# One kernel's hand-written order of steps replaced from end to end: softmax attention with a highway layer, eight batches on one core

## The chip, the cores and the metric

The kernel runs on one NeuronCore of a Trainium2 chip. The metric is the device time of one execution in microseconds; before the change its median is 117.8 us over 3 runs (117.66 to 118.46). A profile is taken of one further execution, and all instruction times below come from it. The engines are named as in the profile: PE (TensorE's matmuls), PEld (its weight loads), DVE (VectorE), ACT (ScalarE), POOL (GpSimd) and SP (the engine that issues most DMAs).

## The reference

```python
q, k, v: (8, 8, 576, 64) float32          # batch, heads, positions, head size
q_s = softmax(q, over the head size)
k_s = softmax(k, over the positions)
kv  = einsum('bhsd,bhse->bhde', k_s, v)   # 64x64 for each head
a   = einsum('bhsd,bhde->bhse', q_s, kv)
x   = a.transpose(0, 2, 1, 3).reshape(4608, 512)
H   = relu(x @ w_h)
T   = sigmoid(x @ w_t + b_t)
out = T * H + (1 - T) * x                 # (4608, 512) float32
```

## The kernel before

The 4608 rows are cut into 36 tiles of 128 rows. A pair of batches makes nine tiles: four of the first batch, four of the second, and one that holds the last 64 rows of both (tile numbers 8, 17, 26 and 35). Each batch has a preparation, and each tile a chain of steps. The program is a flat list of such steps, the string ORDER (line 16 on), written out by hand; the loop at line 502 runs through it and calls one small function for each entry. An entry `mt_17_0` is step mt for tile (or batch) 17, part 0; a letter behind a colon says which engine does it (A is ScalarE, D VectorE, P GpSimd; F joins two halves in one instruction). Nothing else orders the work: each engine executes its own instructions strictly in the order in which the list names them, waits where an operand or a buffer is not ready, and everything behind a waiting instruction on that engine waits too.

Preparation of batch b. `q`, `k`, `v` are loads issued by SP (lines 184, 200, 204, 208); each tensor has three landing buffers, so a load waits until batch b-3 has been consumed. `ek` (line 255) is exp of k, `eq` (300, 304, 309) exp of q, both on ScalarE. `vc` (261) casts v to float16 on GpSimd, ScalarE or VectorE. `kv` (271) accumulates the 64x64 products and the column sums in PSUM, `kr` (283) takes the reciprocals and `kn` (289) writes the normalized block to SBUF, both on VectorE. `qt` (321, 326) transposes exp(q) on TensorE, `qc` (335) copies the result to SBUF. For batch 7 alone, `qd` (342) does this with two DMA transposes.

Chain of tile i. `xu` (363) multiplies the transposed exp(q) with kv. `rs` and `x` (372, 378, VectorE) divide by the row sums. `xt` (386) transposes x on TensorE, `xe` (393) copies it to SBUF on VectorE or ScalarE. `bw` (401 on ScalarE, 403 on TensorE) puts the bias into a PSUM bank, `mt` (413) adds x @ w_t to it, `mh` (421) forms x @ (w_h/2 - I/2) in another bank (the identity is taken from w_h by `whd`, line 228, and the halving is in the cast `whc`, line 234; `wtc`, line 224, casts w_t). `th` (435, 437) is tanh on ScalarE, `dd` (441) is max(gps, -x/2) on VectorE. `uu` forms (tanh+1)*d either in one VectorE instruction (455) or, for tiles marked P, in two GpSimd instructions (452, 453); in the first case the PSUM bank is free only after uu, in the second already after th. `oo` (473, GpSimd) adds x. `st` (481, 489, 493) stores; for most tiles one store takes the halves of two neighbouring tiles. Tiles 0, 4, 5, 6 and 7 do xu to xe and the matmuls in two halves. `fill` (168) are matmuls on zeros that are executed while the first loads are under way.

PSUM's eight banks: two for bw/mt, two for mh (and for the xu of halved tiles), one pair for xu and kv, one for qt, one for the transposes. In SBUF, x has six buffers, d, u, th and the transposed x three each, a pair of output tiles seven, a single output tile three. In the built program each DMA of SP also waits until the eighth DMA before it has landed.

Of the kernel before, what the change touches and what calls it, by code (L numbers as in the profile page):

```python
# [31 lines left out]
uu_6_0:P oo_8_0 oo_6_0 xe_9_0:D mh_7_0 dd_7 bw_7:A mt_7_1 mt_7_0 xu_10_0 xt_12_0 mh_9_0 xe_12_0:D rs_10_0 q_3_0 x_10_0
eq_3_0 eq_3_1 qt_3_2 qc_3_2 dd_9 mh_12_0 xt_10_0 xe_10_0:D qt_3_1 qc_3_1 k_3_0 th_7_0 bw_10:A v_3_0 vc_3_0 xu_11_0
rs_11_0 bw_9:A mt_9_0 ek_3_0 ek_3_2 dd_12 vc_3_2:A x_11_0 qt_3_0 th_9_0 qc_3_0 uu_7_0:P oo_7_0 uu_9_0 mt_10_0 th_10_0
bw_12:A kv_3_0 qt_2_2 q_4_0 qc_2_2:A mh_10_0 eq_4_0:F kr_3_0 kn_3_0 xt_11_0 xe_11_0:D mt_12_0 dd_10 uu_10_0:P oo_9_0
oo_10_0 xu_14_0 rs_14_0 x_14_0 th_12_0 uu_12_0 oo_12_0 mh_11_0 qt_4_0 bw_11:A xu_13_0 rs_13_0 x_13_0 v_4_0 vc_4_0
# [10 lines left out]
dd_21 xt_22_0 xe_22_0 xu_24_0 mt_21_0 mh_22_0 xt_23_0 rs_24_0 qc_6_0 x_24_0 vc_6_0:A kv_6_0 qt_6_1 th_19_0 uu_19_0:P
oo_20_0 q_6_9 dd_22 xe_23_0:D mh_23_0 kr_6_0 th_21_0 uu_21_0 oo_19_0 kn_6_0 bw_22:A mt_22_0 qc_6_1:A dd_23 xu_25_0
rs_25_0 x_25_0 eq_5_2 xt_24_0 qt_5_2 bw_23:A mt_23_0 th_22_0 oo_21_0 uu_22_0:P oo_22_0 qc_5_2:A xu_26_0 xe_24_0
rs_26_0 x_26_0 bw_24:A th_23_0 uu_23_0 xt_25_0 mh_24_0 dd_24 st_10_1 q_7_0 oo_23_0 v_7_0 st_10_0 vc_7_0 vc_7_2 k_7_0  # L50
# [485 lines left out]
```

## Time and profile before

| | before |
|---|---|
| median of 3 runs | 117.8 us (117.66 to 118.46) |
| profiled execution | 117.78 us |
| its span | 116.0 us |
| TensorE's granted clock | 0.99 of full speed |
| data moved | 40.58 MB, 350 GB/s on average |
| DMA issues of loads of 1152 KB | 11.3 (v) and 11.8 us (k) from issue to landing |
| chain that ended last, by engine | PE 54%, POOL 26%, DVE 6%, issue 6% |

The page gives busy time for each engine, the span in 40 equal slices (2.9 us each) with the busy share in tenths, and the DMA queue's share. A matmul's row in the profile lasts longer (379 ns for 512 columns) than the distance to the next one, because matmuls overlap; so TensorE's load is read from the starts. The same holds in a smaller measure for the other engines: a row of 0.68 us on VectorE is followed by the next after 0.60. The timelines give start, duration and, in brackets, the idle time before an instruction and what ended it.

### The profile page before, as it was taken

How to read it: one execution, taken by the hardware profiler on the slowest of the kernel's cores; microseconds unless marked ns; L12 is line 12 of the kernel's file. 1: busy time of each engine (PE TensorE's matmuls, PEld its weight loads, DVE VectorE, ACT ScalarE, POOL GpSimd, SP SyncE). 2: the span in 40 equal slices, each digit the busy share in tenths (PEclk: the TensorE clock that was granted, in tenths of full speed). 3: DMA queues.
4: the chain of work that ended last, by engine and by line, in shares of the span. 5: the costliest groups of instructions: out<-in, count | busy, mean ns of one | idle time of the engine just before them, and what ended most of it. 6: DMA issues, size and time to landing. Idle time of an engine off the chain costs nothing.

```text
span 116.0 us, 3454 instructions
## 1 busy us (share of the span) xinstructions
PE 109.2 (94%) x1355; PEld 62.8 (54%) x1355; DVE 93.7 (81%) x231; ACT 91.2 (79%) x139; POOL 90.9 (78%) x103
## 2 busy tenths in 40 slices
PE   5999999999999999999999999999999999999930
...
DVE  5544678588999999998999899989789869789770
ACT  4354473997999999999999999997999796585620
POOL 5024247089998999999999999986999979999960
...
DMA  2999999999999999999999999999999999894965
GB/s 49 375 397 379 407 391 378 390 377 367 384 384 379 390 393 366 367 393 355 349 386 388 363 401 406 391 384 332 370 398 376 148 276 394 343 364 166 401 257 181
DMA packets 24755, 40.58 MB, mean 350 GB/s; under 512 B 5410, under 2 KB 12834, under 8 KB 24740
## 3 DMA queue, kind: packets, MB, share of 16 engines
...
## 4 chain that ended last, share of the span: by engine, by line
PE 54%; POOL 26%; DVE 6%; issue 6%; DMA 2%; ACT 1%; POOLq 1%; ACTq 0%
POOL o L473 14%; PE gps L421 14%; PE tps L413 13%; PE turned L168 10%; POOL u L453 6%; PE kv L271 4%; PE xu L363 4%; PE turned L386 4%; PE qps L326 3%; POOL g L452 3%; DMA out_dram<-o 2%; POOL v L261 2%; DVE x L378 2%; DVE d L441 2%; DVE xT L393 1%
## 5 line engine op out<-in xcount | busy, mean ns | idle before, releaser
L473 POOL TENSOR_TENSOR o<-u,x 128x512 f32<-128x512 f16 (+1 forms) x36 | 40.5, 1142 | 2.1 <-DVE u L455 1.2
L413 PE MATMUL tps<-w16t,xT 128*128 128x512 f16 (+1 forms) x148 | 37.2, 373 | 0.0
L421 PE MATMUL gps<-w16h,xT 128*128 128x512 f16 x144 | 36.9, 379 | 0.0
L378 DVE TENSOR_TENSOR x<-xu,rs 128x512 f16<-128x512 f32 (+1 forms) x41 | 25.5, 624 | 2.5 <-POOL g L452 0.5
L441 DVE SCALAR_TENSOR_TENSOR d<-x,gps 128x512 f16<-128x512 f16 x36 | 24.1, 677 | 0.5 <-PE gps L421 0.4
L453 POOL TENSOR_TENSOR u<-g,d 128x512 f16<-128x512 f16 x19 | 21.9, 1155 | 1.6
L261 POOL CAST v<-v 128x576 f16<-128x576 f32 (+1 forms) x14 | 12.6, 906 | 11.4 <-DMA v<-in_v_dram 11.3
L255 ACT ACTIVATE ek<-k 128x576 f16<-128x576 f32 (+2 forms) x21 | 18.8, 930 | 2.6 <-DMA k<-in_k_dram 2.5
L413 PEld LDWEIGHTS <-xT 128*128 128x128 f16 x148 | 13.4, 98 | 10.7 <-ACT xT L393 0.2
L421 PEld LDWEIGHTS <-xT 128*128 128x128 f16 x144 | 12.9, 98 | 10.9 <-DVE xT L393 0.8
L401 ACT COPY tps<-ball 128x512 f32<-128x512 f32 x29 | 16.8, 590 | 2.4 <-DVE u L455 2.1
L363 PE MATMUL xu<-kvb,eq 128*128 128x130 f16 (+1 forms) x160 | 15.4, 225 | 0.3 <-DVE x L378 0.2
L363 PEld LDWEIGHTS <-eq 128*128 128x128 f16 (+1 forms) x160 | 10.4, 100 | 8.4 <-DVE x L378 3.6
L386 PE MATMUL turned<-idh,x 128*128 128x128 f16 x144 | 14.5, 220 | 0.1
L309 ACT ACTIVATE qe<-q 128x1024 f16<-128x1024 f32 (+2 forms) x11 | 9.5, 896 | 5.3 <-DMA q<-in_q_dram 5.3
L386 PEld LDWEIGHTS <-x 128*128 128x128 f16 x144 | 10.2, 98 | 6.1 <-DVE x L378 1.6
L455 DVE SCALAR_TENSOR_TENSOR u<-tps,d 128x512 f16<-128x512 f32 (+1 forms) x17 | 11.4, 668 | 2.5 <-ACT tps L437 1.9
L168 PE MATMUL turned<-blank 128*128 128x512 f16 x45 | 12.1, 420 | 1.3 <-POOL blank L150 1.3
L452 POOL TENSOR_SCALAR g<-th 128x512 f16<-128x512 f16 x19 | 11.7, 618 | 1.2 <-DVE x L378 1.2
L435 ACT ACTIVATE th<-tps 128x512 f16<-128x512 f32 x19 | 11.2, 592 | 1.7 <-PE tps L413 1.6
L393 DVE COPY xT<-turned 128x512 f16<-128x512 f16 (+1 forms) x28 | 10.6, 384 | 2.3 <-PE turned L386 2.3
L437 ACT ACTIVATE tps<-tps 128x512 f32<-128x512 f32 (+1 forms) x18 | 10.0, 556 | 2.4 <-PE tps L413 2.4
...
## 6 DMA issues: line engine op xcount, KB each, us to landing
...
k<-in_k_dram SPq DMA_DIRECT2D x5, 1152.0 KB, 11.8
v<-in_v_dram SPq DMA_DIRECT2D x5, 1152.0 KB, 11.3
...
```

Source lines behind the costliest of these rows:

```text
L168: nc.tensor.matmul(spare, blank[:, 0:P], blank, start=True, stop=True, skip_group_check=True)
L255: nc.scalar.activation(t[:, :, c:c + n].rearrange("p j c d -> p c j d"), T[f"k32{b}"][:, c:c + n].rearrange("p c (j d) -> p c j d", j=NJ), ...
L363: nc.tensor.matmul(dst, turned_q(b, jp, n), kvb[b % NKV][:, hh, kk], start=True, stop=True, skip_group_check=True)
L378: nc.vector.tensor_mul(t[:, k0:k1], sums(i, k)[:, :, :, 0:64], T[f"rs{i}_{k}"][:, 0:k1 - k0].unsqueeze(3).to_broadcast([P, k1 - k0, 4, D]))
L386: nc.tensor.matmul(t[:, n], T[f"x{i}"][:, n0 + n % 2:n0 + 2 * P:2], idh, is_transpose=True, start=True, stop=True, skip_group_check=True)
L401: nc.scalar.copy(t[:, cs], ball[:, cs])
L413: nc.tensor.matmul(T[gate(i, k)][:, cs], T[f"xT{i}"][:, n], w16["t"][:, n, cs], start=False, stop=(n == parts[-1] and not first), skip_gro ...
L421: nc.tensor.matmul(t, T[f"xT{i}"][:, n], w16["h"][:, n], start=(first and n == parts[0]), stop=(n == parts[-1] and not (first and len(part ...
L441: nc.vector.scalar_tensor_tensor(t, T[f"x{i}"], -0.5, T[f"gps{i}"], op0=ALU.mult, op1=ALU.max)
L452: nc.gpsimd.tensor_scalar(g, T[f"th{i}"], 1.0, 1.0, op0=ALU.add, op1=ALU.mult)
L453: nc.gpsimd.tensor_mul(t, g, T[f"d{i}"])
L473: eng.tensor_add(t[:, cs], T[f"u{i}_{h}"][:, cs], T[f"x{i}"][:, cs])
```

## The change

Only the string ORDER differs; tiles, loads, halves, buffers and all functions stay. The whole sequence of entries is another one, and for some entries the engine is another one.

- The head: TensorE's fills, the bias product (`bp`) and the DVE set-up now come ahead of the first q; w_h's first half is the second load (it was the ninth); batch 0 begins with heads 2 and 3; k_1_2 and v_1_2 are loaded ahead of q_1_0. There are 46 fills instead of 45.
- vc: 9 on ScalarE (6 before), 11 on GpSimd (14), 2 on VectorE (2). qc: 5 on ScalarE (9), 17 on VectorE (13). xe: 12 on ScalarE (13), 29 on VectorE (28). bw: 29 on ScalarE and 8 on TensorE, as before.
- uu: 19 on GpSimd and 18 on VectorE, as before, but for other tiles (0, 1, 9, 13, 16, 23, 28 move to GpSimd; 2, 6, 10, 14, 17, 30, 33 to VectorE).
- eq_3, eq_5 and ek_3 are joined, eq_4 and ek_5 are split in two.
- SP: five stores come ahead of k_6_0 (three before), q_6_0 comes behind it; q_7_9 comes directly behind q_7_0, v_7_0 directly ahead of the DMA transposes; in the tail st_30, st_21, st_25, st_31, st_33, st_28, st_16_1, st_32, st_34, st_35 is the order.

The diff, cut to its head, some rows in the middle and its end:

```diff
--- before.py
+++ after.py
 ORDER = """
-setuppool q_0_0 v_0_0 fill_8 fill_8 b_32 b_0 eq_0_0 k_0_0 ek_0_0 qt_0_0 setupdve bsplit bp bc fill_8 ek_0_1 vc_0_0:D
-v_0_1 vc_0_1 kv_0_0 kr_0_0 k_0_2 fill_8 ek_0_3 v_0_2 v_0_3 vc_0_2 qc_0_0 kn_0_0 xu_0_0 vc_0_3 ek_0_2 kv_0_1 kr_0_1
-kn_0_1 q_0_4 fill_5 eq_0_1 eq_0_2 xu_1_0 rs_1_0 rs_0_0 x_1_0 x_0_0 fill_8 xt_1_0 xe_1_0:D qt_0_1 w_h_0 whd_1:P whd_0:P
-whc_0:A qc_0_1 xt_0_0 xu_0_1 rs_0_1 x_0_1 bw_1 xe_0_0 xu_3_0 rs_3_0 x_3_0 qt_0_2 bw_0 w_h_2 whd_2:P whd_3:P whc_2:A
-w_t_2 wtc_2:P xt_0_1 mh_0_0 xe_0_1:D xu_2_0 xt_3_0 xe_3_0 rs_2_0 w_t_0 wtc_0:P mh_1_0 q_1_0 mh_0_1 qc_0_2:A x_2_0
-xt_2_0 dd_1 dd_0 k_1_2 eq_1_0 v_1_2 mt_1_0 th_1_0 uu_1_0 vc_1_3 oo_1_0 ek_1_2 ek_1_3 xe_2_0:D mt_0_1 mt_0_0 th_0_0
...
-eq_1_1 xt_5_0 qt_1_1 rs_4_0 x_4_0 mh_5_1 q_2_0 eq_2_0 k_2_2 rs_8_0 xe_5_0:D qc_1_1:A x_8_0 ek_2_3 xt_4_0 xt_4_1
-xe_4_0:D xe_4_1:D mh_5_0 dd_5 mt_5_0 th_5_0 uu_5_0:P k_2_0 ek_2_1 bw_8:A ek_2_2 xu_6_0 rs_6_0 x_6_0 mt_4_1 xt_8_0
-xe_8_0:D xu_6_1 rs_6_1 qt_2_0 x_6_1 xu_7_0 rs_7_0 x_7_0 mt_4_0 xt_6_0 xu_7_1 rs_7_1 xt_6_1 xe_6_0:D xe_6_1:D x_7_1
...
-mt_13_0 dd_13 k_4_0 ek_4_0 ek_4_2 q_4_9 kv_4_0 kr_4_0 kn_4_0 th_14_0 uu_14_0:P bw_17:A th_13_0 uu_13_0 xt_15_0 xe_15_0
-qt_4_1 qc_4_1 mt_17_0 xu_18_0 rs_18_0 x_18_0 oo_14_0 q_5_0 eq_5_0 oo_13_0 v_5_0 vc_5_0 bw_15:A vc_5_2 mh_17_0 xt_16_0
-xe_16_0:D dd_17 eq_4_2 eq_5_1 mt_15_0 th_15_0 xu_20_0 qt_4_2 k_5_0 rs_20_0 x_20_0 mh_15_0 th_17_0 uu_17_0:P oo_17_0
...
-mt_16_0 th_16_0 bw_18:A qt_5_1 kv_5_0 eq_6_0:F dd_16 kr_5_0 kn_5_0 uu_16_0 bw_20:A xt_19_0 mh_18_0 qc_5_1:A st_1_0
...
-mt_20_0 xu_22_0 dd_18 uu_18_0 oo_18_0 st_5_0 st_7_1 q_5_9 st_5_1 xt_21_0 rs_22_0 x_22_0 th_20_0 dd_20 uu_20_0:P
...
-mt_24_0 xe_25_0 eq_6_2 xu_27_0 qt_6_2 xt_26_0 mh_25_0 rs_27_0 x_27_0 xe_26_0:D xu_29_0 rs_29_0 bw_25:A mt_25_0 st_17_0
-eq_7_0:F qd_7_0 qc_6_2:A dd_25 th_24_0 qd_7_1 x_29_0 xt_27_0 xe_27_0 uu_24_0 oo_24_0 mh_26_0 dd_26 xu_30_0 rs_30_0
-th_25_0 x_30_0 st_12_0 uu_25_0:P mh_27_0 bw_27:A mt_27_0 st_14_1 dd_27 xt_30_0 xu_28_0 rs_28_0 q_7_9 st_12_1 bw_26:A
...
-uu_29_0 qc_7_2:A oo_29_0 x_32_0 xe_33_0 mt_31_0 mh_33_0 xt_32_0 bw_33:A th_31_0 dd_31 st_8_0 st_19_0 st_26_0 xu_34_0
-xe_32_0 uu_31_0 rs_34_0 mt_33_0 x_34_0 oo_28_0 st_28_0 st_30_0 oo_31_0 st_31_0 st_25_0 mh_32_0 xu_35_0 dd_33 xt_34_0
-bw_32:A mt_32_0 th_33_0 uu_33_0:P oo_33_0 dd_32 xe_34_0:D mh_34_0 rs_35_0 x_35_0 xt_35_0 bw_34:A th_32_0 uu_32_0 dd_34
-xe_35_0 mt_34_0 th_34_0 uu_34_0 oo_32_0 st_33_0 st_32_0 oo_34_0 st_34_0 bw_35_0 mh_35_0 dd_35 mt_35_0 th_35_0 uu_35_0
-oo_35_0 bw_35_1 mt_35_1 st_35_0 th_35_1 uu_35_1 oo_35_1:D st_35_1:A
+setuppool fill_8 b_0 fill_8 b_32 setupdve bsplit bp fill_8 fill_8 q_0_0 w_h_0 v_0_2 vc_0_2:D whd_1:P eq_0_0 qt_0_0
+k_0_2 whd_0:P whc_0:A v_0_3 vc_0_3:A ek_0_3 ek_0_2 kv_0_1 kr_0_1 fill_8 v_0_1 k_0_0 ek_0_1 qc_0_0 kn_0_1 xu_0_1 rs_0_1
+x_0_1 v_0_0 vc_0_1 ek_0_0 vc_0_0:A kv_0_0 q_0_4 eq_0_2 eq_0_1 fill_6 kr_0_0 kn_0_0 xu_0_0 xt_0_1 rs_0_0 x_0_0 xu_1_0
+rs_1_0 xe_0_1 x_1_0 qt_0_1 xt_0_0 qc_0_1 bc bw_0 bw_2 xe_0_0 xt_1_0 w_h_2 whd_2:P mh_0_0 whd_3:P whc_2:A xu_2_0
+xe_1_0:D rs_2_0 x_2_0 mh_0_1 dd_0 mh_1_0 w_t_2 wtc_2:P w_t_0 wtc_0:P xt_2_0 xe_2_0 qt_0_2 xu_3_0 rs_3_0 mt_0_1 mt_0_0
+mh_2_0 k_1_2 ek_1_2 th_0_0 dd_1 x_3_0 mt_2_0 ek_1_3 v_1_2 vc_1_2:A vc_1_3:D uu_0_0:P oo_0_0 q_1_0 dd_2 xt_3_0 xe_3_0:D
...
+rs_4_0 xu_8_0 rs_8_0 x_4_0 qt_1_1 q_2_0 eq_2_0 qc_1_1:A xt_5_0 xe_5_0:D x_8_0 k_2_0 ek_2_1 ek_2_0 mh_5_1 xt_4_0 xt_4_1
+xe_4_1:D mh_5_0 xe_4_0:D dd_5 mt_5_0 th_5_0 xt_8_0 xu_6_1 rs_6_1 x_6_1 mt_4_1 xu_6_0 k_2_2 v_2_2 vc_2_2 ek_2_2 vc_2_3
+mt_4_0 th_4_0 bw_8:A rs_6_0 x_6_0 xu_7_0 ek_2_3 rs_7_0 x_7_0 xe_8_0:D qt_2_0 mh_4_1 mh_4_0 qc_2_0 xt_6_1 xt_6_0 xu_7_1
+xe_6_1:D rs_7_1 xe_6_0:D mt_8_0 xt_7_0 kv_2_1 v_2_0 vc_2_0 vc_2_1:A kv_2_0 dd_4 x_7_1 xt_7_1 uu_5_0:P kr_2_0 oo_5_0
...
+xu_17_0 rs_17_0 x_17_0 qt_4_1 v_4_0 vc_4_0 xt_13_0 xe_13_0:D mh_14_0 th_10_0 ek_4_0 uu_10_0 oo_10_0 dd_14 q_4_9 q_5_0
+k_5_0 vc_4_2 st_1_1 v_5_0 st_3_0 q_6_9 st_5_1 st_3_1 xu_15_0 rs_15_0 x_15_0 st_1_0 xt_17_0 mh_13_0 bw_13:A bw_14:A
+mt_14_0 xe_17_0 ek_4_2 th_14_0 k_6_0 q_5_9 v_6_0 st_5_0 dd_13 xu_16_0 rs_16_0 x_16_0 xt_15_0 mt_13_0 th_13_0 xe_15_0:D
+bw_17:A kv_4_0 qc_4_1 uu_11_0:P oo_11_0 eq_5_0:F uu_14_0 uu_13_0:P oo_14_0 kr_4_0 kn_4_0 oo_13_0 bw_15:A xt_16_0
+xe_16_0:D mh_17_0 dd_17 mt_17_0 xu_18_0 rs_18_0 x_18_0 th_17_0 uu_17_0 vc_5_2 oo_17_0 mh_15_0 mt_15_0 xt_18_0 xu_20_0
...
+oo_23_0 xe_26_0:D bw_25:A th_24_0 eq_7_2 mh_24_0 eq_7_0:F v_7_0 qd_7_0 qd_7_1 x_27_0 mt_25_0 dd_24 uu_24_0 oo_24_0
+vc_7_0 xu_30_0 mh_26_0 rs_30_0 x_30_0 xt_27_0 xe_27_0:D st_14_1 mh_25_0 xu_28_0 dd_26 th_25_0 rs_28_0 xt_30_0 dd_25
+uu_25_0:P oo_25_0 x_28_0 bw_27:A mt_27_0 st_19_0 st_12_0 st_12_1 st_14_0 st_8_0 st_23_0 xe_30_0:D bw_26:A mt_26_0
...
+dd_31 bw_33:A mt_31_0 th_31_0 uu_28_0:P st_30_0 oo_28_0 xu_34_0 rs_34_0 xt_32_0 xe_32_0:D x_34_0 uu_31_0 st_21_0
+oo_31_0 st_25_0 st_31_0 mh_33_0 mt_33_0 xu_35_0 dd_33 rs_35_0 th_33_0 uu_33_0 xt_34_0 xe_34_0:D bw_32:A mh_32_0
+mt_32_0 mh_34_0 oo_33_0 bw_34:A st_33_0 x_35_0 dd_32 th_32_0 uu_32_0 xt_35_0 mt_34_0 th_34_0 xe_35_0:D mh_35_0 st_28_0
+st_16_1 oo_32_0 st_32_0 bw_35_0 bw_35_1 mt_35_0 dd_34 uu_34_0 oo_34_0 st_34_0 th_35_0 mt_35_1 th_35_1 dd_35 uu_35_0
+oo_35_0 st_35_0 uu_35_1 oo_35_1:D st_35_1:A
 """
```

More of the change, by code (lines that the diff above doesn't have):

```diff
@@ L22 @@
-xt_2_0 dd_1 dd_0 k_1_2 eq_1_0 v_1_2 mt_1_0 th_1_0 uu_1_0 vc_1_3 oo_1_0 ek_1_2 ek_1_3 xe_2_0:D mt_0_1 mt_0_0 th_0_0
-qt_1_0 qc_1_0 mh_3_0 bw_2 mt_2_0 vc_1_2:A kv_1_1 uu_0_0 oo_0_0 th_2_0 bw_3 mt_3_0 k_1_0 ek_1_1 ek_1_0 dd_3 kr_1_1
-v_1_0 vc_1_0 vc_1_1:A kn_1_1 xu_5_1 th_3_0 rs_5_1 x_5_1 mh_2_0 dd_2 uu_2_0:P uu_3_0:P oo_2_0 oo_3_0 xt_5_1 xu_4_1
-kv_1_0 kr_1_0 rs_4_1 bw_5 kn_1_0 xe_5_1 mt_5_1 x_4_1 q_1_4 eq_1_2 xu_5_0 rs_5_0 qt_1_2 qc_1_2 bw_4 xu_4_0 xu_8_0 x_5_0
-eq_1_1 xt_5_0 qt_1_1 rs_4_0 x_4_0 mh_5_1 q_2_0 eq_2_0 k_2_2 rs_8_0 xe_5_0:D qc_1_1:A x_8_0 ek_2_3 xt_4_0 xt_4_1
@@ L27 @@
-xe_4_0:D xe_4_1:D mh_5_0 dd_5 mt_5_0 th_5_0 uu_5_0:P k_2_0 ek_2_1 bw_8:A ek_2_2 xu_6_0 rs_6_0 x_6_0 mt_4_1 xt_8_0
-xe_8_0:D xu_6_1 rs_6_1 qt_2_0 x_6_1 xu_7_0 rs_7_0 x_7_0 mt_4_0 xt_6_0 xu_7_1 rs_7_1 xt_6_1 xe_6_0:D xe_6_1:D x_7_1
-mt_8_0 ek_2_0 v_2_0 vc_2_0:D qc_2_0 mh_4_1 mh_4_0 xt_7_0 dd_4 xt_7_1 th_4_0 vc_2_1 kv_2_0 v_2_2 vc_2_3 vc_2_2:A kv_2_1
-kr_2_1 mh_8_0 bw_6:A mh_6_1 th_8_0 mt_6_1 kr_2_0 oo_5_0 kn_2_1 uu_4_0:P kn_2_0 xu_9_0 dd_8 q_2_4 eq_2_2 eq_2_1 xe_7_1
-uu_8_0:P oo_4_0 rs_9_0 x_9_0 mt_6_0 xe_7_0 qt_2_1 qc_2_1 th_6_0 mh_6_0 dd_6 mh_7_1 xt_9_0 xu_12_0 rs_12_0 x_12_0
@@ L32 @@
[L32 to L36, printed above, removed]
@@ L37 @@
-xt_14_0 xe_14_0:D vc_4_2:A bw_14:A mt_11_0 th_11_0 xu_17_0 rs_17_0 x_17_0 qc_4_0:A xt_13_0 mh_14_0 dd_11 uu_11_0:P
-oo_11_0 xu_15_0 rs_15_0 xe_13_0:D x_15_0 mt_14_0 dd_14 mh_13_0 xu_16_0 rs_16_0 x_16_0 bw_13:A xt_17_0 xe_17_0:D
-mt_13_0 dd_13 k_4_0 ek_4_0 ek_4_2 q_4_9 kv_4_0 kr_4_0 kn_4_0 th_14_0 uu_14_0:P bw_17:A th_13_0 uu_13_0 xt_15_0 xe_15_0
-qt_4_1 qc_4_1 mt_17_0 xu_18_0 rs_18_0 x_18_0 oo_14_0 q_5_0 eq_5_0 oo_13_0 v_5_0 vc_5_0 bw_15:A vc_5_2 mh_17_0 xt_16_0
-xe_16_0:D dd_17 eq_4_2 eq_5_1 mt_15_0 th_15_0 xu_20_0 qt_4_2 k_5_0 rs_20_0 x_20_0 mh_15_0 th_17_0 uu_17_0:P oo_17_0
@@ L42 @@
-xt_18_0 mh_16_0 xu_19_0 dd_15 qc_4_2 xe_18_0:D rs_19_0 qt_5_0 qc_5_0 bw_16:A ek_5_0:F xt_20_0 x_19_0 q_6_0 xe_20_0:D
-mt_16_0 th_16_0 bw_18:A qt_5_1 kv_5_0 eq_6_0:F dd_16 kr_5_0 kn_5_0 uu_16_0 bw_20:A xt_19_0 mh_18_0 qc_5_1:A st_1_0
-st_1_1 mh_20_0 st_3_0 uu_15_0:P oo_15_0 xe_19_0:D xu_21_0 rs_21_0 x_21_0 oo_16_0 mt_18_0 th_18_0 k_6_0 st_3_1 v_6_0
-mt_20_0 xu_22_0 dd_18 uu_18_0 oo_18_0 st_5_0 st_7_1 q_5_9 st_5_1 xt_21_0 rs_22_0 x_22_0 th_20_0 dd_20 uu_20_0:P
-xe_21_0:D st_7_0 qt_6_0 mh_19_0 xu_23_0 rs_23_0 x_23_0 vc_6_2 dd_19 bw_19:A bw_21:A mt_19_0 ek_6_0 ek_6_2 mh_21_0
@@ L47 @@
[L47 to L50, printed above, removed]
-mt_24_0 xe_25_0 eq_6_2 xu_27_0 qt_6_2 xt_26_0 mh_25_0 rs_27_0 x_27_0 xe_26_0:D xu_29_0 rs_29_0 bw_25:A mt_25_0 st_17_0
@@ L52 @@
-eq_7_0:F qd_7_0 qc_6_2:A dd_25 th_24_0 qd_7_1 x_29_0 xt_27_0 xe_27_0 uu_24_0 oo_24_0 mh_26_0 dd_26 xu_30_0 rs_30_0
-th_25_0 x_30_0 st_12_0 uu_25_0:P mh_27_0 bw_27:A mt_27_0 st_14_1 dd_27 xt_30_0 xu_28_0 rs_28_0 q_7_9 st_12_1 bw_26:A
-mt_26_0 st_14_0 st_23_0 st_16_0 st_16_1 xe_30_0:D mh_30_0 ek_7_0 oo_25_0 x_28_0 xt_28_0 xe_28_0:D ek_7_2 kv_7_0
-xt_29_0 th_26_0 uu_26_0 oo_26_0 th_27_0 uu_27_0:P mh_28_0 bw_30:A mt_30_0 kr_7_0 kn_7_0 xu_31_0 st_21_0 bw_28:A
-mt_28_0 dd_30 xe_29_0:D rs_31_0 dd_28 th_30_0 uu_30_0:P mh_29_0 x_31_0 xt_31_0 xe_31_0:D oo_27_0 oo_30_0 bw_29:A
@@ L57 @@
-xu_33_0 eq_7_2 th_28_0 rs_33_0 uu_28_0 mt_29_0 qt_7_2 bw_31:A mh_31_0 x_33_0 xt_33_0 xu_32_0 th_29_0 dd_29 rs_32_0
-uu_29_0 qc_7_2:A oo_29_0 x_32_0 xe_33_0 mt_31_0 mh_33_0 xt_32_0 bw_33:A th_31_0 dd_31 st_8_0 st_19_0 st_26_0 xu_34_0
-xe_32_0 uu_31_0 rs_34_0 mt_33_0 x_34_0 oo_28_0 st_28_0 st_30_0 oo_31_0 st_31_0 st_25_0 mh_32_0 xu_35_0 dd_33 xt_34_0
-bw_32:A mt_32_0 th_33_0 uu_33_0:P oo_33_0 dd_32 xe_34_0:D mh_34_0 rs_35_0 x_35_0 xt_35_0 bw_34:A th_32_0 uu_32_0 dd_34
-xe_35_0 mt_34_0 th_34_0 uu_34_0 oo_32_0 st_33_0 st_32_0 oo_34_0 st_34_0 bw_35_0 mh_35_0 dd_35 mt_35_0 th_35_0 uu_35_0
@@ new lines @@
+xe_1_0:D rs_2_0 x_2_0 mh_0_1 dd_0 mh_1_0 w_t_2 wtc_2:P w_t_0 wtc_0:P xt_2_0 xe_2_0 qt_0_2 xu_3_0 rs_3_0 mt_0_1 mt_0_0
+mh_2_0 k_1_2 ek_1_2 th_0_0 dd_1 x_3_0 mt_2_0 ek_1_3 v_1_2 vc_1_2:A vc_1_3:D uu_0_0:P oo_0_0 q_1_0 dd_2 xt_3_0 xe_3_0:D
+th_2_0 uu_2_0 oo_2_0 qc_0_2 bw_1 mt_1_0 kv_1_1 bw_3 kr_1_1 kn_1_1 eq_1_0 qt_1_0 qc_1_0 k_1_0 mh_3_0 ek_1_0 ek_1_1
+xu_5_1 rs_5_1 x_5_1 v_1_0 vc_1_0:A th_1_0 mt_3_0 th_3_0 dd_3 xt_5_1 vc_1_1 kv_1_0 xe_5_1:D kr_1_0 xu_4_1 rs_4_1 bw_5
+kn_1_0 uu_1_0:P mt_5_1 x_4_1 bw_4 q_1_4 uu_3_0:P oo_1_0 oo_3_0 eq_1_2 qt_1_2 qc_1_2 xu_5_0 rs_5_0 x_5_0 eq_1_1 xu_4_0
```

20 lines of the change are left out of this document (added).

## Prediction

> **What bounds the kernel now.** I read the page first (busy time, the slices), then busy time by stage, then TensorE's timeline, the waits of its weight loads, and the DMA issues with ScalarE's timeline near the last loads.
>
> The page: four engines and the DMA are all nearly full, so busy shares alone name no bound.
>
> ```profile
> PE 109.2 (94%) x1355; PEld 62.8 (54%) x1355; DVE 93.7 (81%) x231; ACT 91.2 (79%) x139; POOL 90.9 (78%) x103
> ...
> PE   5999999999999999999999999999999999999930
> ...
> DVE  5544678588999999998999899989789869789770
> ACT  4354473997999999999999999997999796585620
> POOL 5024247089998999999999999986999979999960
> ...
> DMA  2999999999999999999999999999999999894965
> ```
>
> By stage (columns: length, then busy time of PE, PEld, DVE, ACT, POOL, clock, DMA share, GB/s): until 30 us the three elementwise engines have room, from 30 to 90 none has, after 105 all run dry.
>
> ```profile
> 0.00:20.00 20.00, 18.34 (x179) 9.40 (x180) 11.61 (x40) 9.94 (x14) 7.29 (x18) 1.00 0.93 338
> 20.00:30.00 10.00, 9.96 (x137) 5.21 (x135) 7.80 (x23) 8.63 (x15) 6.28 (x9) 1.00 1.06 378
> 30.00:60.00 30.00, 29.90 (x452) 18.47 (x451) 28.08 (x71) 29.22 (x43) 28.60 (x30) 1.00 1.07 377
> 60.00:90.00 30.00, 29.81 (x382) 18.00 (x379) 26.87 (x60) 28.11 (x42) 27.96 (x29) 1.00 1.05 381
> ...
> 105.00:116.00 11.00, 6.21 (x46) 3.11 (x43) 6.59 (x13) 3.88 (x8) 6.91 (x7) 0.89 0.69 264
> ```
>
> TensorE's timeline (start, duration, line): the starts tell it. Four xu matmuls, four transposes and four mt matmuls follow at 0.24, 0.22 and 0.86 us, that is 59, 56 and 216 ns for each, and nowhere closer. Then kv waits 0.27 us: 59.07 less 57.94 is 1.13, not 0.86.
>
> ```profile
> 57.48 0.40 PE L363 MATMUL xu<-kvb,eq 128*128 128x130 f16 x4
> 57.72 0.39 PE L386 MATMUL turned<-idh,x 128*128 128x128 f16 x4
> 57.94 1.03 PE L413 MATMUL tps<-w16t,xT 128*128 128x512 f16 x4
> 59.07 0.77 PE L271 MATMUL kv<-v,ek 64*64 64x65 f16 x72
> ```
>
> I add TensorE's work by these spacings: 284 mh and mt at 216 ns (and 8 halves at 109), 160 xu at 59, 272 transposes at 56, kv at 0.50 or 0.80 us a step, 45 fills and the bias matmuls at 216: 105.3 us. At 28.71 (xu_5_0) 81.1 us of it are left; the last matmul group starts at 110.61 and is through at 111.1. So in 82.4 us TensorE lost only 1.3, and 0.27 (before 59.07) and 0.36 (before 79.36) of that are visible waits. **TensorE's stream is the bound from about 20 us on; before that the loads are.** An order can win back at most what is lost: little.
>
> The last loads, and the stores: ScalarE waits for batch 7's k until 91.85, and SP holds the stores back until 105.01.
>
> ```profile
> 88.33 3.80 SPq L342 DMA_TRANSPOSE eq<-qe  x2
> ...
> 101.66 0.55 SPq L481 DMA_DIRECT2D out_dram<-o  x1
> 105.01 7.44 SPq L489 DMA_DIRECT2D out_dram<-o  x7
> ```
> ```profile
> 91.85 2.22 ACT L255 ACTIVATE ek<-k 128x1152 f16<-128x1152 f32 x2 [0.64 <-DMA k<-in_k_dram]
> ```
>
> **The sum's base.** The profiled execution took 117.78 us, its span is 116.00, so 1.78 lie around it; the median of the runs is 117.80, the same. One per cent (1.2 us) is about what a measurement of this kernel tells from no change.
>
> **The change part by part.**
>
> *Casts, copies, biases.* The counts of bias copies (29 on ScalarE), of th and of u forms (18 on VectorE, 19 on GpSimd) stay; only tiles swap, so by duration they cost nothing. GpSimd loses two 576-wide v casts (666 ns) and one 1152-wide (1146 ns): -2.5 us. ScalarE gains them (+2.5), loses four 256-wide qc (369 ns) and one half xT copy (366 ns) and has one more joined eq (-0.2): +0.4. VectorE gains four qc of 285 ns and one 273 ns copy: +1.4. On the path: nothing, since TensorE's stream covers all of it (its busy time is 29.9 of 30); were the cover gone, ScalarE's +0.4 and VectorE's +1.4 would count. One fill more is 0.22, before the first loads are used up, hidden.
>
> *Loads and steps up to 30 us.* w_h's first half goes from ninth place to second, heads 2 and 3 of batch 0 come first, q_1_0 goes behind k_1_2 and v_1_2. Sizes by the code: 0.52 MB for w_h_0 or q_0_0, 0.29 a v piece, 0.59 a k pair. Up to the first half of w_h and all of batch 0 both orders move the same 4.06 MB (in use from 13.92), up to w_t_0 the same 5.63 (its cast starts at 19.11 and ends at 20.15). mt_0_0 thus can't start before 20.2 in either order; by then 89.2 us of TensorE's work are left before and 88.9 after. I followed the steps after it: v_1_2 now lands some 1.4 us earlier, q_1_0 at 23.55, where v_1_2 landed (GpSimd's cast), so eq_1_0 runs 23.6 to 24.7 on ScalarE, qt_1_0 starts at 24.8, and TensorE waits about 0.5, where it lost 0.4 before. xu_5_0 starts at 28.85 with 80.8 left, against 28.71 with 81.1: -0.2. Bounds: TensorE lost 1.3 between 20 and 30; none of it, or all of it again: -1.3 to +1.3. I take -0.2, the sum followed.
>
> *30 to 90 us.* The two visible waits (0.63) have their causes moved. kv_4 waited for ek_4_2 on ScalarE: TensorE had 51.5 us of its work left at kv_4, ScalarE 42.5 after ek_4_2, 9.0 less; in the new order these are 50.8 and 42.9, so ScalarE has 1.1 us more time. kv_6 waited for x_24 on VectorE (through at 79.22): 31.6 and 28.3 before, 32.0 and 30.3 after, 1.6 us more time. Both waits go: -0.6. Next late is bw_8: behind qc_1_1, three ek_2, th_5 and th_4 on ScalarE (0.89 + 3 x 0.58 + 2 x 0.50 + 0.52 = 4.15, from 30.9 to 35.1), while mt_8 could start at 34.8: +0.3. GpSimd's v casts for batches 3 to 5, followed the same way, end 0.5 to 2.6 us ahead of kv. Waits that such sums don't show: from 0 to 2.3 (all TensorE lost between 15 and 30, the stage with most hand-offs); I take 0.3, nearer to the stage 30 to 60, with 0.27 visible.
>
> *Batch 7's loads.* v_7_0 goes behind k_7_0 on SP's queue, q_7_9 ahead of both. Between v_1_2 (7.34 MB, 23.55) and k_7_0 (32.90 MB, 91.85) the queue delivered 0.374 MB/us; v_7_0 now ends at 33.03 MB: 92.2 us, where k_7_0 ends at 31.85 (89.0). vc_7_0 (GpSimd) and vc_7_2 (ScalarE) each take 1.15, kv_7 starts at 93.4; TensorE, with 17.5 us of work left and an end at 110.3 if nothing else were lost (111.1 - 0.2 - 0.6), would be ready at 92.8: +0.6. Bounds: 0 (0.6 earlier) to 1.6 (one more microsecond of queue).
>
> *SP's queue and the end.* Five stores instead of three now stand ahead of k_6_0 (0.5 MB more), but q_6_0 (1.05) moves behind it, so k_6_0 ends at 25.8 MB instead of 26.2. In the tail st_30_0 waits for oo_30 with st_21, st_25, st_28 and st_16_1 queued behind it; 6.8 MB follow the DMA transposes (through about 94.7) and need 18.1 us at that rate: 112.8, as late as the last issue before (112.80). Nobody on the compute side waits but oo_34 and oo_35, for buffers of st_31 and st_33 (107 to 109): hidden. I take +0.1, bounds 0 to +1.5 (no slack is left in the queue).
>
> Sum: -0.2 - 0.6 + 0.3 + 0.3 + 0.6 + 0.1 = +0.5; 117.8 + 0.5 = **118.3 us**.
>
> A rule against this reading. The Trainium skill, "Perfetto Trace Analysis", section "Identifying the Most-Contended Engine", says that matmul busy time is a poor measure of the distance to TensorE's limit and that the weight loads' busy share should be used. Here that share is 54%; by it TensorE has nearly half its time free. This case's starts disagree (216 ns a matmul, group after group, no gap), so the sum by the trace is 118.3; by the rule it would be the time of rival 4.
>
> **Rivals.**
>
> 1. *ScalarE falls behind from 75 us on (slower).* From the end of eq_2_0 (30.8) to the end of vc_7_2 it now has 58.5 us of work by its spacings (22 th, 22 bias copies, 9 ek, the rest). Before, 53.1 us of such work took until 88.2, that is 57.4, a factor of 1.08; at that pace vc_7_2 ends at 94.0 and kv_7 is 1.2 late, 0.6 more than the sum has; bw_30, bw_29 and xe_29 behind it (1.5 us) make mt_30 and mt_29 wait again, 0.5; and at mt_23, where ScalarE has 0.4 us less time than before, 0.4: 118.3 + 1.5 = 119.8. It decides once vc_7_2 ends after 93.4. For it: ScalarE is busy 29.2 of 30. Against: part of the 8% were waits for TensorE.
> 2. *The stores collide (slower).* Should eq_7_0 end after 91, SP runs dry and the transposes land after 97; 6.8 MB then end at 115: +2.3, 120.1. Against: eq_7_0 has 53.8 us of work from 30.8, so it ends between 84.6 and 88.9.
> 3. *All waits vanish (faster).* The head wins 0.7, the 1.3 of lost time goes to 0.3 and v_7 lands in time: 117.8 - 1.7 = 116.1. For it: VectorE has about 1 us more time than before at most steps that TensorE waits for. Against: it wants zero waits in 80 us.
> 4. *TensorE has room.* PEld is busy only 62.8 of 116; should matmuls go closer together than 216 ns once others feed them in time, the queue bounds: 40.58 MB at 0.374 are 108.5, from 2 us, and 2 more for the last landing, with 1.78 around: 114.3.
>
> **How the numbers follow.** Forecast 0.47, the likeliest, with its own range of 117.2 to 119.0; ScalarE 0.28; stores and other collisions 0.12; vanished waits 0.11; room 0.02. Faster by over 1% (below 116.6): 0.02 and 0.10 of the vanished waits: 0.12. Slower by over 1% (above 119.0): 0.24 of the ScalarE case, 0.12 of the stores, 0.05 of the forecast's upper end: 0.41. Within: 0.47. The range from 116.8 to 120.9 reaches into the ScalarE and store cases and to the edge of the faster one.
>
> **What would show it.** Right: xu_5_0 near 28.9; the group of mt_8 starts about 0.3 late; vc_7_2 waits for DMA until about 92; TensorE's last group ends near 111.6; no wait before kv_4 and kv_6; SP's stores without a gap after 95. Wrong: waits of weight loads on ScalarE after 60 us above 1 us (rival 1), DMA slices below 9 before 90 us (rival 2), a last matmul before 110 (rivals 3 and 4).

## The result, and the profile after

The new order is slower: 119.4 us median over 6 runs (119.12 to 119.84) against 117.9 over 6 runs of the kernel before (117.66 to 118.46), a ratio of 1.0126 with a 95% interval of 1.0098 to 1.0155. The profiled execution's span is 117.6 us (116.0 before). The prediction said 118.3 and a range of 116.8 to 120.9; the time lies in the range, 1.1 us above the forecast and outside its "within 1%".

The page of the kernel after, its counterpart to the lines shown of before (busy time by engine; the span in 40 slices of 2.9 us):

```profile
PE 109.2 (93%) x1356; PEld 62.6 (53%) x1356; DVE 94.9 (81%) x236; ACT 91.0 (77%) x136; POOL 88.9 (76%) x100
...
PE   5999999999999589999999999999999999999930
...
ACT  4337792978995499998989999999999995665320
...
DMA  3999999999999999999999999999995889939785
```

Busy times moved about as worked out (POOL -2.0 for -2.5, DVE +1.2 for +1.4, ACT -0.2 for +0.4), and TensorE's is the same 109.2. What is new is a dip in TensorE's row, the 5 and 8 in slices 14 and 15 (38.2 to 44.1 us), and a 5 and a 4 in ScalarE's row, one slice sooner. Everything else of TensorE is as full as before. Busy time by stage (columns as in the prediction's table) puts a number on it:

```profile
20.00:30.00 10.00, 9.80 (x135) 4.95 (x134) 8.49 (x24) 8.32 (x15) 6.91 (x9) 1.00 1.07 372
30.00:60.00 30.00, 28.44 (x379) 17.52 (x379) 26.51 (x69) 26.69 (x39) 26.31 (x28) 1.00 1.07 377
60.00:90.00 30.00, 29.99 (x443) 18.06 (x442) 27.18 (x61) 29.26 (x43) 29.02 (x30) 1.00 1.05 377
```

From 30 to 60 us TensorE is busy 28.44 instead of 29.90, and ScalarE 26.7 instead of 29.2. TensorE's timeline there (start, duration, line; in brackets the idle time and what ended it) has one hole:

```profile
39.08 0.40 PE L363 MATMUL xu<-kvb,eq 128*128 128x130 f16 x4
39.32 0.59 PE L421 MATMUL gps<-w16h,xT 128*128 128x512 f16 x2
41.46 0.62 PE L326 MATMUL qps<-idh,qe 128*128 128x128 f16 x8 [1.55 <-ACT qe L309]
41.92 0.59 PE L421 MATMUL gps<-w16h,xT 128*128 128x512 f16 x2
```

In the kernel before, the same transposes (L326) follow their forerunners at the usual spacing:

```profile
39.18 0.59 PE L413 MATMUL tps<-w16t,xT 128*128 128x512 f16 x2
39.62 0.61 PE L326 MATMUL qps<-idh,qe 128*128 128x128 f16 x8
```

After the change, two mh matmuls from 39.32 are through by their usual spacing at 39.75; the next group, qt_2_1, starts at 41.46. That is 1.71 us lost at one place, and the transposes wait for exp(q) of batch 2 (`eq`, L309). Why is exp(q) late? ScalarE's timeline:

```profile
36.58 0.58 ACT L401 COPY tps<-ball 128x512 f32<-128x512 f32 x1
39.77 0.37 ACT L393 COPY xT<-turned 128x256 f16<-128x256 f16 x1 [2.61 <-DVE xT L393]
40.04 1.36 ACT L309 ACTIVATE qe<-q 128x256 f16<-128x256 f32 x2
```

ScalarE stands still for 2.61 us ahead of a copy of 0.37 us, xe_7_1, the second half of tile 7's transposed x. It waits for VectorE's write of the same tile, xe_7_0, although the two copies read and write different columns (line 393). What it reads was there: in e2 below, both copies run from 37.56. The exps behind it could have started some 2.1 us sooner: e1 below starts them at 37.91, when their q has landed, and in the kernel before, where they stand first, they start at 37.73:

```profile
36.56 0.58 ACT L401 COPY tps<-ball 128x512 f32<-128x512 f32 x1
37.08 0.59 ACT L435 ACTIVATE th<-tps 128x512 f16<-128x512 f32 x1
37.73 1.36 ACT L309 ACTIVATE qe<-q 128x256 f16<-128x256 f32 x2
39.01 0.63 ACT L393 COPY xT<-turned 128x256 f16<-128x256 f16 x2
```

And VectorE, after, comes to xe_7_0 only behind the kv normalization and dd_8:

```profile
37.36 0.24 DVE L283 RECIPROCAL rz<-kv 128x2 f32<-128x2 f32 x2 [0.46 <-PE kv L271]
37.56 1.20 DVE L289 TENSOR_TENSOR kvb<-kv,rz 64x128 f16<-64x128 f32 x4
38.79 0.69 DVE L441 SCALAR_TENSOR_TENSOR d<-x,gps 128x512 f16<-128x512 f16 x1
39.40 0.28 DVE L393 COPY xT<-turned 128x256 f16<-128x256 f16 x1
```

So two edits of the change meet: xe_7_0 went from ScalarE to VectorE, behind dd_8 there, and xe_7_1 went ahead of the exps on ScalarE. The exps feed qt_2_1, which stands in TensorE's queue, as it did before, ahead of work that was ready.

Summed over all matmuls (distance from start to start, less the usual one for that shape), TensorE's lost time rose by 1.28 us: -0.12 up to 30 us, +1.47 from 30 to 60, -0.17 from 60 to 90, +0.10 after. The gap alone is 1.71; all else together is -0.43. With the one fill more (0.22) that makes 1.5, and the last matmul starts that much later (112.42 instead of 110.93).

### The profile page after: what moved, and what is told of

Same layout as the page of the kernel before. It is cut to its first block, busy times and chain, and to the rows that moved or that the text cites. A ratio compares the mean times of both kernels' runs of the same rounds, so it can differ in the third digit from the quotient of the medians.

```text
span 117.6 us, 3455 instructions
## 1 busy us (share of the span) xinstructions
PE 109.2 (93%) x1356; PEld 62.6 (53%) x1356; DVE 94.9 (81%) x236; ACT 91.0 (77%) x136; POOL 88.9 (76%) x100
## 4 chain that ended last, share of the span: by engine, by line
PE 77%; DVE 7%; DMA 5%; ACT 4%; SPq 2%; POOL 1%; issue 1%; DVEq 0%; ACTq 0%
PE gps L421 24%; PE tps L413 24%; PE xu L363 8%; PE turned L386 7%; DMA v<-in_v_dram 5%; PE kv L271 5%; PE qps L326 4%; PE turned L168 3%; PE qps L321 2%; DVE u L455 2%; DVE d L441 1%; ACT qe L309 1%; ACT tps L437 1%; ACT ek L255 1%; POOL o L473 1%
## 5 line engine op out<-in xcount | busy, mean ns | idle before, releaser
L261 POOL CAST v<-v 128x1152 f16<-128x1152 f32 (+1 forms) x11 | 10.1, 926 | 5.3 <-DMA v<-in_v_dram 5.3
L309 ACT ACTIVATE qe<-q 128x1024 f16<-128x1024 f32 (+2 forms) x10 | 9.4, 968 | 3.2 <-DMA q<-in_q_dram 3.2
L372 DVE RECIPROCAL rs<-xu 128x8 f32<-128x8 f32 (+1 forms) x41 | 8.0, 197 | 4.3 <-PE xu L363 3.7
```

## Experiments

The theory: this one stall is the whole loss. Its rivals: the later loads and stores set the end, so a gap at 40 us is absorbed; ScalarE is overloaded in the last third; the new head costs. All ratios below are to the kernel before on the same chip, with their 95% intervals.

**The exps first (e1).** One entry of the changed order moves:

```diff
-xe_7_1 q_2_4 eq_2_2 eq_2_1 qt_2_1
+q_2_4 eq_2_2 eq_2_1 xe_7_1 qt_2_1
```

> The changed order with one entry moved: xe_7_1 (ScalarE's half copy of tile 7) goes behind eq_2_2 and eq_2_1 instead of ahead of them. Theory: the 1.2 to 1.7 us that the changed order lost are one stall, ScalarE standing 2.61 us in xe_7_1 for VectorE's xe_7_0 with the exps of q_2 behind it, so that qt_2_1 starts 1.71 us late; with the exps first that gap goes, but v_7's late load, so far hidden by it, shows up with 0.3 to 0.6: 117.8 to 118.4, ratio to before 1.000 to 1.005. Rival (the end is set by the later loads and the stores, the gap at 40 us is absorbed): no change, 119.2 to 119.6. Rival (ScalarE's load in the last third): gap gone at 40 us, but new waits of weight loads on ScalarE after 75 us, 119 or more.

Measured: 118.17 us, 1.0000 (0.9979 to 1.0021). The exps start at 37.91 and TensorE's transposes follow the two mh matmuls from 39.84 without a gap; the wait of xe_7_1 is still there, but now it hurts nobody:

```profile
37.91 1.36 ACT L309 ACTIVATE qe<-q 128x256 f16<-128x256 f32 x2 [0.65 <-DMA q<-in_q_dram]
40.43 0.37 ACT L393 COPY xT<-turned 128x256 f16<-128x256 f16 x1 [1.16 <-DVE xT L393]
```
```profile
40.27 0.61 PE L326 MATMUL qps<-idh,qe 128*128 128x128 f16 x8
```

**The other engine (e2).** The order stays, only `xe_7_0:D` becomes `xe_7_0` (ScalarE does both halves).

> The changed order with one engine changed: xe_7_0 on ScalarE, as in the kernel before, in its new place ahead of xe_7_1; the exps of q_2 stay behind both. Theory: ScalarE no longer waits for VectorE, both half copies (0.37 us each) run as soon as xt_7_1 is through, the exps start at about 38.0 instead of 40.04, and the gap of 1.71 us shrinks to 0 to 0.4: 117.8 to 118.6. If it isn't the wait but the place of the exps behind any copy that costs, the gap stays above 1 us and the time at 119 or more.

Measured: 118.16 us, 1.0003 (0.9984 to 1.0022). The copies stand ahead of the exps as in the changed order, but ScalarE waits for the transposes alone:

```profile
37.56 0.65 ACT L393 COPY xT<-turned 128x256 f16<-128x256 f16 x2 [0.39 <-PE turned L386]
38.09 1.37 ACT L309 ACTIVATE qe<-q 128x256 f16<-128x256 f32 x2
```

**Sooner on VectorE (e6).** Neither ScalarE's order nor the engine changes; xe_7_0 moves in VectorE's queue:

```diff
-kv_2_0 dd_4 ... mt_6_1 xe_7_0:D mt_6_0
+kv_2_0 xe_7_0:D dd_4 ... mt_6_1 mt_6_0
```

> The changed order with only the place of xe_7_0 on VectorE changed: ahead of dd_4 instead of behind dd_8 (four instructions and the rest between them, some 2.5 us sooner); ScalarE's order stays, xe_7_1 still ahead of the exps. Theory: what counts is when VectorE writes its half, not which engine or which order; xe_7_1 waits at most 0.5 us, the exps start at about 38, the gap before qt_2_1 shrinks to below 0.4: 118.0 to 118.5. Rival (any copy on VectorE that ScalarE's copy waits for costs the stall): 119 or more.

Measured: 118.25 us, 1.0016 (0.9998 to 1.0034). VectorE copies at 36.50, xe_7_1 runs at 38.10 and the exps at 38.37. Three edits that have nothing in common but that the exps no longer stand behind this wait give the same time; it is the wait, not the engine and not the order by itself.

**The stall put into the kernel before (e3).**

```diff
-dd_8 q_2_4 eq_2_2 eq_2_1 xe_7_1 ... mt_6_0 xe_7_0 qt_2_1
+dd_8 xe_7_0:D xe_7_1 q_2_4 eq_2_2 eq_2_1 ... mt_6_0 qt_2_1
```

> The kernel before with only the suspected cause put in: xe_7_0 on VectorE behind dd_8, and xe_7_1 on ScalarE ahead of eq_2_2 and eq_2_1; everything else as before. Theory: the exps of q_2 start late again, qt_2_1 is late by 1 to 1.7 us and the whole time goes up by as much: 118.9 to 119.5, ratio 1.009 to 1.015. Rival (the new order as a whole, not this stall, costs the time): at most 0.3 us, below 118.2.

Measured: 119.67 us, 1.0133 (1.0094 to 1.0172): the old order with this alone is as slow as the new one. TensorE's hole is back at the same place:

```profile
39.21 0.59 PE L413 MATMUL tps<-w16t,xT 128*128 128x512 f16 x2
41.45 0.62 PE L326 MATMUL qps<-idh,qe 128*128 128x128 f16 x8 [1.65 <-ACT qe L309]
```

**The new head alone (e8).** The changed order's entries up to xu_5_0, then the rest as before.

> The changed order's entries up to xu_5_0 (the loads and steps of the first 29 us), then the rest in the order of the kernel before. Tests the head by itself, which the prediction put at -0.2 (bounds -1.3 to +1.3). Theory: 117.6 to 118.1, ratio 0.996 to 1.000, since the lost time of TensorE up to 30 us differs by only 0.2 to 0.5 in the profiles. Rival (the new head costs time that the body's gains hide): 118.5 or more; rival (the head gains, the body loses as much): below 117.5.

Measured: 118.00 us, 0.9999 (0.9980 to 1.0017). By the interval, the new head of 29 us neither wins nor loses more than about 0.2 us.

**v_7 sooner, the stall left in (e4).** `v_7_0` moves from behind eq_7_0 to ahead of k_7_0 on SP's queue.

> The changed order with v_7_0 put back ahead of k_7_0 on SP's queue, the stall at 40 us left in. Theory: with TensorE 1.7 us late already, the later load of v_7 was hidden (kv_7 had only 0.06 us of wait beyond its usual spacing), so nothing is gained: 119.2 to 119.6, ratio to before 1.010 to 1.015. Rival (the load order of batch 7 is the cost, as the prediction had it with 0.6): 118.4 to 118.9.

Measured: 119.28 us, 1.0106 (1.0070 to 1.0143), nothing gained, as the theory said.

**v_7 sooner, without the stall (e5 with the exps first, e7 with xe_7_0 on ScalarE).**

> The changed order with both edits: the exps of q_2 ahead of xe_7_1, and v_7_0 ahead of k_7_0 on SP's queue. Theory: without the stall TensorE arrives at kv_7 early enough to wait for v_7; the earlier load takes that wait away, 0.1 to 0.4 us less than the run with the exps first alone (118.17): 117.8 to 118.1, ratio to before 0.997 to 1.001. Rival (v_7's load never mattered): the same as that run within 0.1 us.

> The changed order with xe_7_0 on ScalarE and v_7_0 ahead of k_7_0. Theory: the run with xe_7_0 on ScalarE showed 0.38 us before kv_7 where 0.09 are usual; the earlier load of v_7 takes the 0.28 away: 117.8 to 118.1, ratio 0.997 to 1.000. Rival: later loads of k_7 push ek_7 back and give the gain away, 118.1 to 118.4.

Measured: 119.81 us, 1.0164 (1.0119 to 1.0209), and 119.92 us, 1.0172 (1.0128 to 1.0217). Both expectations fell, and so did their rivals (that of e7 had the mechanism, k_7 pushed back, but not its size): the edit that was free in e4 costs 1.7 us here. ScalarE's timeline of e7:

```profile
88.58 1.11 ACT L401 COPY tps<-ball 128x512 f32<-128x512 f32 x2
92.33 2.22 ACT L255 ACTIVATE ek<-k 128x1152 f16<-128x1152 f32 x2 [2.64 <-DMA k<-in_k_dram]
94.45 1.14 ACT L261 CAST v<-v 128x1152 f16<-128x1152 f32 x1
```

Now k_7 comes last, and both exps of it (2.22) and the v cast (1.14) stand behind its landing on ScalarE; with v last, the exps fill the time until it lands and only the cast is left. TensorE reaches kv_7 at 93.1 and gets its second half at 95.64:

```profile
92.24 1.03 PE L421 MATMUL gps<-w16h,xT 128*128 128x512 f16 x4
93.55 0.48 PE L271 MATMUL kv<-v,ek 64*64 64x65 f16 x36 [0.28 <-ACT ek L255]
95.64 0.48 PE L271 MATMUL kv<-v,ek 64*64 64x65 f16 x36 [1.61 <-ACT v L261]
```

In e4 TensorE comes 2.1 us later, at 95.2, and ScalarE takes k_7 at 91.76 without waiting:

```profile
90.72 1.11 ACT L401 COPY tps<-ball 128x512 f32<-128x512 f32 x2
91.76 2.21 ACT L255 ACTIVATE ek<-k 128x1152 f16<-128x1152 f32 x2
93.88 1.14 ACT L261 CAST v<-v 128x1152 f16<-128x1152 f32 x1
```

So the stall at 40 us and this wait at 94 us cost about the same and don't add: the earlier one hides the later.

**The DMA transposes behind four stores (e9 on e2, e10 on e7).** `qd_7_0 qd_7_1` move behind st_14_1, st_19_0, st_12_0 and st_12_1 on SP's queue.

> The changed order with xe_7_0 on ScalarE, and SP's two DMA transposes of batch 7 behind st_14_1, st_19_0, st_12_0 and st_12_1 instead of ahead of them. In the runs without the stall eq_7_0 ends at 88.1 instead of 90.2, the transposes' 256-byte packets begin at 89.5 while the last load (v_7) is still landing, the load's packets fall from 40 to 3 in half a microsecond, and v_7 lands at 92.3; where the stall is left in, the transposes begin at 91.0 or later and the load is through by 90.6. Theory (the transposes hold up the load's last packets): behind four stores they come later, v_7 lands near 90.7, the 0.28 at kv_7 goes: 117.7 to 118.0, ratio 0.996 to 1.000. Rival (the last load just takes until 92.3): v_7 lands as late as before, 118.1 to 118.3; rival (the transposes are then late for xu_31): 118.5 or more.

> The run with xe_7_0 on ScalarE and v_7_0 ahead of k_7_0 (119.92), with the two DMA transposes behind the same four stores. There k_7 landed at 92.3 and ScalarE's ek_7 (2.2) and vc_7_2 (1.15) came after it, so that kv_7 waited 1.8 in its middle. Theory (the transposes hold up the last load, whichever it is): k_7 lands near 90.7, ek_7 ends at 92.9 and vc_7_2 at 94.0, the wait shrinks by about 1.6: 118.1 to 118.5, ratio 1.001 to 1.005. Rival (loading v_7 first makes k_7 late by itself): 119.6 to 120.

Measured: 118.90 us, 1.0061 (1.0041 to 1.0081), and 119.78 us, 1.0135 (1.0110 to 1.0161). The theory fell: v_7 in e9 is used at 92.37 and k_7 in e10 at 92.39, no sooner. What e9 loses is its second rival: xu_31 waits 0.87 us at 96.6 for the later transposes. SP still issues the first transpose at 88.19, but the four stores now stand ahead of it in the queue:

```profile
83.67 1.24 SPq L493 DMA_DIRECT2D out_dram<-o  x2
88.19 7.18 SPq L342 DMA_TRANSPOSE eq<-qe  x2
```

So the edit did what it was meant to do: the transposes' first packet (they move 256 bytes a packet, the load 2304) goes at 91.76 in e9 and 91.64 in e10, against 89.49 in e2 and 89.38 in e7.

**Sixteen fills fewer (e11 on e2, e12 on e7).**

```diff
-bp fill_8 fill_8 q_0_0 ... kr_0_1 fill_8 v_0_1 ... eq_0_1 fill_6
+bp fill_8 q_0_0 ... kr_0_1 fill_4 v_0_1 ... eq_0_1 fill_2
```

> The changed order with xe_7_0 on ScalarE (118.16) and 30 fills instead of 46 (8 fewer ahead of q_0_0, 4 fewer behind kr_0_1, 4 fewer behind eq_0_1). The late transposes did not move the last load's landing, so that reading fell. New reading: a 16 KB transfer of the queue called instruction takes 1.1 us of one DMA engine; in the runs without the stall it starts at 88.8 to 89.9, ahead of that engine's last packets of v_7 or k_7, and the load is complete only at 91.7 to 91.9; where it starts at 90.2 or later, the load is complete by 90.5 to 91.4. It comes when TensorE has issued about 2,270 matmuls and weight loads (2,260 to 2,274 in eight runs of this order), so it is taken to be TensorE's own code. Sixteen fills fewer are 32 such instructions fewer ahead of it: it moves to about 91.1. Theory: v_7 is complete by 90.6, POOL's cast starts at 91.2 without waiting, the 0.28 at kv_7 goes: 117.7 to 118.1 if the fills don't count otherwise. Rival (the load's last packets are late for another reason): v_7 as late as before, 118.1 to 118.3. If TensorE's clock falls for want of fills, the head gets longer and the time rises by that; the trace shows it apart.

> The run with xe_7_0 on ScalarE and v_7_0 ahead of k_7_0 (119.92) with the same 30 fills instead of 46. There k_7 came last, ScalarE's ek_7 waited for it until 92.3 and kv_7 lost 1.8. Theory (TensorE's code transfer holds up one DMA engine): it moves to about 91.1, behind the load; k_7 is complete by 90.6, ek_7 ends at 92.8 and vc_7_2 at 93.9, kv_7 loses 0.2 to 0.6 instead of 2.2 in all: 118.2 to 118.6, plus what the head may lose. Rival (another reason): 119.8 to 120.

Measured: 117.97 us, 0.9996 (0.9980 to 1.0011), and 119.81 us, 1.0149 (1.0129 to 1.0169). The time of e11 lies in the theory's range, but not by its mechanism, and that of e12 is its rival's. The 16 KB transfer moved as expected (from 88.8 to 90.6 and 90.2), and the load's last packets ended at 90.8 and 90.4 instead of 91.8. But the casts and exps did not start sooner. ScalarE in e11:

```profile
89.81 2.21 ACT L255 ACTIVATE ek<-k 128x1152 f16<-128x1152 f32 x2
92.62 1.15 ACT L261 CAST v<-v 128x1152 f16<-128x1152 f32 x1 [0.60 <-DMA v<-in_v_dram]
```

So the transfer does hold up packets, but taking that away is not enough. The packets and semaphores in the traces show why. A load counts as landed once its semaphore has been raised 16 times, once for each DMA engine, and each raise follows from a packet of 4 bytes behind that engine's data. For the last load (k_7 or v_7), in us:

| run | 16 KB transfer starts | last data packet ends | transposes' first packet | raises after 91.5 | last raise | load in use |
|---|---|---|---|---|---|---|
| e4 | 90.22 | 90.50 | 91.51 | 0 of 16 | 90.97 | 91.76 |
| e2 | 88.81 | 91.76 | 89.49 | 10 | 92.27 | 92.30 |
| e7 | 88.83 | 91.78 | 89.38 | 10 | 92.31 | 92.33 |
| e9 | 88.78 | 91.92 | 91.76 | 1 | 92.35 | 92.37 |
| e10 | 88.80 | 91.94 | 91.64 | 1 | 92.37 | 92.39 |
| e11 | 90.56 | 90.77 | 89.55 | 10 | 92.60 | 92.62 |
| e12 | 90.22 | 90.44 | 89.44 | 9 | 92.26 | 92.28 |

The table shows two hold-ups, and each alone keeps the load until about 92.3. In e9 and e10 the transposes come behind the load, 15 raises are there by 91.22 and 90.93, and the last one belongs to the packets that the 16 KB transfer made late. In e11 and e12 the transfer comes late enough, but the transposes begin while the load still moves: some of their packets then take up to 2.3 us, the last of these ends at 92.46 and 92.12, and from there on the missing raises arrive within 0.15 us. In e4 the stall has pushed both behind the load, no packet of a transpose takes over 0.1 us, and k_7 is there before ScalarE asks for it. So e9 and e10 took away one hold-up and e11 and e12 the other. No run takes away both without the stall, and why packets of a transpose delay the raises of a load is **open**. No version beats the kernel before: the best, e11, takes the same time.

## Why the prediction was right in its range and wrong in its size

By the terms of its own sum (+0.5, measured +1.5 between the medians):

- **Waits that such sums don't show**: taken as 0.3 with bounds of 0 and 2.3; measured 1.71, one wait. This is the term that was mis-sized. The step behind it is the one on casts and copies: the prediction priced the half copies that change engine by duration alone (366 ns less on ScalarE, 273 ns more on VectorE) and put them "on the path" at nothing, because TensorE's stream covers all of it. It followed the v casts, kv_4, kv_6 and bw_8 along their engines' queues, but not this copy. The order itself shows which work stands behind which; that the second half waits for the first, only the traces show. e1, e2 and e6 each let the exps start by 38.4 and have none of the loss; e3 puts the wait in and has the whole loss.
- **The head**: -0.2 taken, 0.0 +- 0.2 by e8. In the profile TensorE's lost time up to 30 us falls by 0.12 and the one fill more adds 0.22. Right as far as the runs can tell.
- **The waits before kv_4 and kv_6 go**: -0.6 taken. They shrank, from 0.27 to 0.17 and from 0.36 to 0.15, that is -0.3. Some 0.09 of each can't go: it comes ahead of kv wherever nothing is late. TensorE around kv_4, after (before it was 57.94 to 59.07, 1.13 for four matmuls, now 1.03):

```profile
60.37 1.03 PE L413 MATMUL tps<-w16t,xT 128*128 128x512 f16 x4
61.40 0.78 PE L271 MATMUL kv<-v,ek 64*64 64x65 f16 x72
```
- **bw_8**: +0.3 taken, 0 measured; mt_8 starts at 35.29 in its group without a gap.
- **v_7**: +0.6 taken (v usable at 92.2, TensorE ready at 92.8, kv_7 at 93.4). In the kernel after 0.06: TensorE, late by the stall, comes at 94.8. GpSimd's half of the cast waits 0.18 for v, until 92.60, and ScalarE takes k_7 and v_7 without a wait for either:

```profile
91.33 2.21 ACT L255 ACTIVATE ek<-k 128x1152 f16<-128x1152 f32 x2
93.45 1.14 ACT L261 CAST v<-v 128x1152 f16<-128x1152 f32 x1
```

  In e2, without the stall, v is usable at 92.3 and kv_7 loses 0.38 at 93.2, 0.28 more than its usual 0.09. The wait was real and its size half of what was said; it was hidden by another that was not foreseen. That its time was right is luck: the prediction took it from the rate of the queue, scaled from k_7's 91.85 in the kernel before, while the data are through by 90.5 in e4 and e12 and the two hold-ups add the rest. Already k_7's 91.85 had such a part: 15 of its 16 raises come by 90.58, the last at 91.83.
- **The queue and the tail**: +0.1 taken, 0.08 measured (from TensorE's last matmul to the end of the span it is 4.87 instead of 4.79). SP's stores do have a gap, from 101.7 to 104.4, where none was expected, as they wait for oo_30; the kernel before had it from 102.2 to 105.0, and nobody waits for it. SP's timeline of the kernel after:

```profile
89.80 3.53 SPq L342 DMA_TRANSPOSE eq<-qe  x2
...
100.29 1.36 SPq L481 DMA_DIRECT2D out_dram<-o  x2
104.42 6.46 SPq L489 DMA_DIRECT2D out_dram<-o  x6
```

Of the rivals, the first (ScalarE falls behind from 75 us on, 119.8) has nearly the right time and the right engine but not the place: after 60 us TensorE's weight loads wait for ScalarE only 0.5 us in all, where its sign was more than 1, and e1, with ScalarE's load unchanged, has the old time. The second (stores collide) did not come: eq_7_0 ends at 89.8 and the transposes have landed by 95.3, although the DMA row has the slice below 9 (a 5, from 88.2 to 91.1 us) that was named as its sign. The third (all waits vanish) did not come. The fourth fell: without a stall groups still follow at 216 ns a matmul. The Trainium skill, "Perfetto Trace Analysis", section "Identifying the Most-Contended Engine", judges TensorE's headroom by the weight loads' busy share, beside the share of peak FLOPs, which is not worked out here. The trace disagrees on the first: PEld is busy 53%, and the matmul groups start without a gap.

The three fixed versions (1.0000, 1.0003, 1.0016) also say what the rest of the reordering is worth: nothing that these runs can tell (their intervals lie between 0.9979 and 1.0034). With TensorE's stream full from 20 us on, this order could lose much at one place and win little anywhere.
